# A 7x7 convolution by short transforms on one core: the weight transform as row-tiled pairs of 49-row matmuls

## Chip, core and metric

The kernel runs on one core of a Trainium2 chip. The metric is the device time of one execution in microseconds (us); less is better. TensorE is called PE in the profile (its weight loads PEld), VectorE DVE, ScalarE ACT, GpSimd POOL, and SyncE, which here only issues transfers, SP.

## The reference

The reference convolves an image x of 224 x 224 pixels and 96 channels (bf16) with a 7 x 7 filter w of 96 x 96 channels. It does so circularly, by Fourier transforms over the image plane:

```python
wp = jnp.pad(w, ((0, H - K), (0, W - K), (0, 0), (0, 0)))
Xf = rfft2(x.astype(float32), axes=(1, 2))
Wf = rfft2(wp.astype(float32), axes=(0, 1))
Yf = jnp.einsum('bhwi,hwio->bhwo', Xf, Wf)
y = irfft2(Yf, s=(H, W), axes=(1, 2)).astype(bfloat16)
```

The output has the shape of x.

## The kernel before

**The method.** The kernel doesn't use the large transform. Along the height it cuts the image into 8 blocks of 28 rows, each with 6 rows of halo, and takes a real transform of length 34 in each block: 17 frequencies, s = 0 to 16. Along the width it convolves directly, with 7 taps, two output columns at a time, in a form that replaces products by sums of inputs and sums of taps. So the weights are needed once per frequency, per part (up to three combinations of the real and imaginary part; such a combination is a "slot", 50 in all) and per tap or sum of taps (10), as matrices of 96 x 96: the tensor WF, [96 input channels, 50 slots, 10 taps, 96 output channels].

**The stages.**

1. Transform of x (`a_jobs`, `f_jobs`): matmuls with strips of x as weights and the table Fm moving, copied out of PSUM into xf.
2. Transform of w (`prep_jobs`): makes WF from w. This is the stage that the change rewrites.
3. Sums of the transformed inputs (`jit`), on VectorE, into J.
4. Products (`b_round`): for each strip t (seven strips of 32 image columns) and each frequency s, 36 or so matmuls of 96 rows, with J or xf as weights and WF moving. ScalarE, VectorE and GpSimd combine the results into yf, which goes to a scratch tensor in DRAM.
5. Back transform (`c_jobs`): reads the scratch, matmuls with the table Gm, copies to yo, stores the output.

**The transform of w.** SP loads w as a matrix wq with one row per tap position (49 rows, PW) and 96 x 96 columns (input channel times output channel). A second copy lies right below it, at row 49, shifted by half the output channels (48 columns), so that wq has 98 rows (PW2). For an output channel o, the weights of a matmul are the columns o, o + 96, o + 192 and so on: 128 columns with a step of 96 elements, of which the first 96 are the input channels. Columns past the matrix hold the table Em and zeros, so that these extra reads meet defined numbers. The moving operand is Em, a table of sine values times a mask over taps. It has two halves: half 0 is zero in rows 49 to 97, half 1 is zero in rows 0 to 48. One matmul with all 98 rows (line 332) so makes the columns of output channel o from the upper copy and of o + 48 from the lower. The slots are made in six groups (PGRP). Group 0 (two frequencies) is made with 49-row matmuls of 50 moving columns, eight to a PSUM bank. Groups 1 to 5 (three frequencies each) take 98-row matmuls of 120 columns, four to a bank, so 48 matmuls and 12 banks per group. After each bank, `evac` copies 480 elements per partition into WF, choosing VectorE or ScalarE by a running estimate of their loads. The third slot of a frequency isn't made by a matmul; it is the difference of two others (`diff`), on VectorE.

**What sets the order.** All instructions of an engine run in the order in which they are written; the wrapper `_Ordered` (lines 76 to 91) sees to it, and all of them carry the number of its line 86 in the profile. The prologue (lines 651 to 665) runs 16 jobs of the x transform, four of group 0, and then mixes them. Groups 1 to 5 are lists of jobs that `pace` (line 673) feeds into `b_round` at two points of each round, so that a list is used up evenly between a first and a last point:

```python
for gi in range(1, len(PGRP)):
    add(2 * PGRP[gi - 1][0], 2 * PGRP[gi - 1][1] - 1, prep_jobs(gi))
```

A list of a group has 12 matmul jobs (one bank each) and then three differences. PSUM has eight banks, which all jobs and rounds take in turn (`bank`); a round takes two.

**The tables.** Lines 209 to 265 compute Fm and Em. GpSimd makes the index ramps and zeroes the end of wq (line 232). VectorE reduces the angles, ScalarE takes the sines (`sin_q`), GpSimd masks the first (lines 240 and 241), and VectorE writes Fm (line 256), after it has computed the tap mask mk and its two halves mk2 (lines 252 to 255). Then it writes Em (lines 263 to 265). On SP the transfers are queued in this order: the first strips of x, the first copy of w, two more strips of x, the second copy of w (lines 176 to 185). A dummy matrix wu of zeros feeds 24 matmuls that keep TensorE busy from 1.05 us on.

Of the kernel before, what the change touches and what calls it, by code (L numbers as in the profile page):

```python
# [10 lines left out]
ALU = mybir.AluOpType  # L11
ACTF = mybir.ActivationFunctionType

KT = 7
# [11 lines left out]
NB = 8  # L26
POS = TW + HALO
NTAP = 10
TAPS = ((7, 8, 9, 6), (0, 2, 4, 6), (1, 3, 5))
NSLOT = 2 + 3 * (NS - 1)  # L30
# [18 lines left out]
def slot(s, part):  # L49
    return part if s == 0 else 2 + 3 * (s - 1) + part  # L50
# [3 lines left out]
def kernel(  # L54
# [7 lines left out]
    _, H, W, C = x.shape  # L62
# [4 lines left out]
    R = HB + PAD  # L67
    PW = KT * KT
    FR = 2 * NS
    PW2 = 2 * PW  # L70
    C2 = C // 2
    CG = ((0, 3), (3, 3), (6, 2))
    SYNC = mybir.DependencyInfo(mybir.DependencyClass.Sync, mybir.DependencyReason.DATA)
# [19 lines left out]
    VE, SE, GE, TE, DE = (_Ordered(e) for e in (nc.vector, nc.scalar, nc.gpsimd, nc.tensor, nc.sync))  # L93
# [9 lines left out]
    def bank():  # L103
        return pools["psb"].tile([128, 512], F32, name="pb")
# [5 lines left out]
    def apart(key, zone, r):  # L110
        for z, q in parts.setdefault(key, []):
            if z != zone and q.engine != r.ins.engine:
                tc.declare_no_dep(r.ins, q, reason="disjoint parts of one tile")
        parts[key].append((zone, r.ins))
        return r

    def evac(out_ap, in_ap, n):
        if tail[0]:
            return tail_evac(out_ap, in_ap, n)
        cv, ca = 180 + 1.0 * n, 160 + 0.85 * n  # L120
        if load["v"] + cv <= load["a"] + ca:
            load["v"] += cv
            return VE.tensor_copy(out=out_ap, in_=in_ap)
        load["a"] += ca
        return SE.copy(out=out_ap, in_=in_ap)

    def tail_evac(out_ap, in_ap, n):
        tail[0] += 1
        return VE.tensor_copy(out=out_ap, in_=in_ap) if tail[0] % 2 else SE.copy(out=out_ap, in_=in_ap)

    def dma(out_ap, in_ap):
        return DE.dma_start(out=out_ap, in_=in_ap)

    WF = cpool.tile([128, NSLOT, NTAP, C], BF16, name="WF")
# [4 lines left out]
    Fm = cpool.tile([R, 2, NS, JG], BF16, name="Fm")  # L139
# [9 lines left out]
    stmp = stmp_cm.__enter__()  # L149
    wqx = wtmp.tile([128, C - 1 + 127 * C + 1], BF16, name="wq")  # L150
    wq = wqx[0:PW2]
    Em = wqx[0:PW2, C * C:C * C + 2 * NSLOT * NTAP].rearrange("p (h a t) -> p h a t", h=2, a=NSLOT)
    XHW = PAD * C + 32
    xh_bufs = [J_bufs[2][0:R, i * XHW:(i + 1) * XHW] for i in range(2)]
    for xb in xn_bufs:
# [13 lines left out]
    def load_x(c):  # L169
        t, k = divmod(c, 4)  # L170
        h, jg = divmod(k, 2)
        load_rows(xn_bufs[c % NXN], jg, t * 2 * TW + h * PXC, PXC)

    wsrc = w.rearrange("kh kw i o -> (kh kw) (i o)")
# [5 lines left out]
    for h in range(2):  # L180
        if h:
            for c in range(2, NXN):
                load_x(c)
        for p0, p1 in ((0, 48), (48, PW)):
            dma(wq[h * PW + p0:h * PW + p1, 0:C * C - h * C2], wsrc[p0:p1, h * C2:])

    wu = cpool.tile([128, 128], BF16, name="wu")
    wur = wu[:].unsqueeze(1).to_broadcast([128, 4, 128])
# [8 lines left out]
    def ftile(shape):  # L197
        ntmp[0] += 1
        return stmp.tile(shape, F32, name=f"ct{ntmp[0]}")
# [4 lines left out]
    def floor_div(out_ap, in_ap, d):  # L204
        VE.tensor_scalar(out=out_ap, in0=in_ap, scalar1=1.0 / d, scalar2=-(d - 1) / (2.0 * d), op0=ALU.mult, op1=ALU.add)
        VE.tensor_single_scalar(out=out_ap, in_=out_ap, scalar=MAGIC, op=ALU.add)
        VE.tensor_single_scalar(out=out_ap, in_=out_ap, scalar=MAGIC, op=ALU.subtract)
# [2 lines left out]
    VE.memset(pi_t[:], math.pi)  # L210
    dmy = ftile([128, 1])
    SE.activation(out=dmy[:], in_=pi_t[:], func=ACTF.Sin, bias=0.0, scale=0.0)

    def sin_q(q):
        fl = ftile(list(q.shape))
        floor_div(fl[:], q, Q)
        VE.scalar_tensor_tensor(out=q, in0=fl[:], scalar=-float(Q), in1=q, op0=ALU.mult, op1=ALU.add)
        return SE.activation(out=q, in_=q, func=ACTF.Sin, bias=pi_t[:q.shape[0], :], scale=-2.0 * math.pi / Q)

    a2 = ftile([R, NS, 2]); ph2 = ftile([R, NS, 2]); nrj = ftile([R, JG])  # L220
    a3 = ftile([PW2, NS, 2]); ph3 = ftile([PW2, NS, 2])
    pw_i = ftile([PW2, 1]); thp = ftile([PW2, 1]); twp = ftile([PW2, 1]); hf = ftile([PW2, 1])
    twc = ftile([PW2, KT]); mk = ftile([PW2, NTAP]); mk2 = ftile([PW2, 2, NTAP])
    iota(a2[:], [[2, NS], [0, 2]])
    iota(ph2[:], [[0, NS], [17, 2]], base=17)
    iota(nrj[:], [[-B, JG]], cm=1)
# [2 lines left out]
    iota(ph3[:], [[0, NS], [-17, 2]], base=17)  # L229
    iota(twc[:], [[1, KT]])  # L230

    GE.memset(wqx[0:PW2, C * C + 2 * NSLOT * NTAP:], 0.0)
    VE.memset(a2[:, 0, 1:2], 34.0)
    VE.memset(ph2[:, 0, 1:2], 17.0)
    VE.tensor_scalar(out=nrj[:], in0=nrj[:], scalar1=0.0, scalar2=float(L - 1), op0=ALU.max, op1=ALU.min)
    qf = ftile([R, JG, NS, 2])
# [5 lines left out]

    VE.memset(a3[:, 0, 1:2], 34.0)
    VE.memset(ph3[:, 0, 1:2], 17.0)
    VE.tensor_single_scalar(out=hf[:], in_=pw_i[:], scalar=float(PW), op=ALU.is_ge)
    VE.scalar_tensor_tensor(out=pw_i[:], in0=hf[:], scalar=-float(PW), in1=pw_i[:], op0=ALU.mult, op1=ALU.add)
    floor_div(thp[:], pw_i[:], KT)
    VE.scalar_tensor_tensor(out=twp[:], in0=thp[:], scalar=-float(KT), in1=pw_i[:], op0=ALU.mult, op1=ALU.add)
    qe = ftile([PW2, NS, 2])
    VE.scalar_tensor_tensor(out=qe[:], in0=a3[:], scalar=thp[:, 0:1], in1=ph3[:], op0=ALU.mult, op1=ALU.add)  # L250
    sin_q(qe[:])
    VE.tensor_scalar(out=mk[:, 0:KT], in0=twc[:], scalar1=twp[:, 0:1], scalar2=None, op0=ALU.is_equal)
    VE.tensor_tensor(out=mk[:, KT:NTAP], in0=mk[:, 0:6:2], in1=mk[:, 1:6:2], op=ALU.add)
    VE.tensor_scalar(out=mk2[:, 1], in0=mk[:], scalar1=hf[:, 0:1], scalar2=None, op0=ALU.mult)
    VE.tensor_tensor(out=mk2[:, 0], in0=mk[:], in1=mk2[:, 1], op=ALU.subtract)
    VE.tensor_copy(out=Fm.rearrange("p r s j -> p j s r"), in_=qf[:])
    pe3 = ftile([PW2, NSLOT])
    pv = pe3[:, 2:].rearrange("p (s r) -> p s r", r=3)
    VE.tensor_copy(out=pe3[:, 0:2], in_=qe[:, 0, :])
# [1 line left out]
    VE.tensor_tensor(out=pv[:, :, 1], in0=qe[:, 1:, 1], in1=qe[:, 1:, 0], op=ALU.subtract)  # L261
    VE.tensor_tensor(out=pv[:, :, 2], in0=pv[:, :, 0], in1=pv[:, :, 1], op=ALU.subtract)
    for k0, k1 in ((0, slot(PGRP[0][1], 0)), (slot(PGRP[0][1], 0), NSLOT)):
        VE.tensor_tensor(out=Em[:, :, k0:k1], in0=pe3[:, k0:k1].unsqueeze(1).unsqueeze(3).to_broadcast([PW2, 2, k1 - k0, NTAP]),
                         in1=mk2[:].unsqueeze(2).to_broadcast([PW2, 2, k1 - k0, NTAP]), op=ALU.mult)

    def build_g(nj):
        PG = nj * FR
# [36 lines left out]
    def prep_jobs(gi):  # L305
        s0, s1 = PGRP[gi]
        ns = s1 - s0
        full = gi == 0
        if full:
            ncol = NSLOT_OF(s0, s1) * NTAP  # L310
        else:
            ncol = 2 * ns * NTAP
        nb = C // NB
        hb = NB // 2
        assert NB * ncol <= 512 and C2 % hb == 0

        def mk_(ob):
            def f():
                pw = bank()
                if full:  # L320
                    pv_ = pw[:, 0:NB * ncol].rearrange("p (o q) -> p o q", q=ncol)
                    ev = Em[0:PW, 0, slot(s0, 0):slot(s0, 0) + ncol // NTAP, :].rearrange("p a t -> p (a t)")
                    for k in range(NB):
                        o = ob * NB + k
                        TE.matmul(pv_[:, k], lhsT=wqx[0:PW, o:o + 127 * C + 1:C], rhs=ev, start=True, stop=True)
                    wv = WF[0:C, slot(s0, 0):slot(s0, 0) + ncol // NTAP].rearrange("i a t o -> i (a t) o")
                    apart(("W", gi), ob // 2, evac(wv[..., ob * NB:(ob + 1) * NB], pv_[0:C].rearrange("i o q -> i q o"), NB * ncol))
                    return
                pv_ = pw[:, 0:NB * ncol].rearrange("p (k h q) -> p k h q", h=2, q=ncol)
                ev = Em[:, :, slot(s0, 0):slot(s1 - 1, 2) + 1, :].rearrange("p h (s r) t -> p h s (r t)", r=3)[:, :, :, 0:2 * NTAP]  # L330
                for k in range(hb):
                    o = ob * hb + k
                    TE.matmul(pv_[:, k], lhsT=wqx[0:PW2, o:o + 127 * C + 1:C], rhs=ev, start=True, stop=True)
                pv_ = pv_[0:C]
                o0, o1 = ob * hb, (ob + 1) * hb
                wv = WF[0:C, slot(s0, 0):slot(s1 - 1, 2) + 1].rearrange("i (s r) t (h o) -> i s (r t) h o", r=3, h=2)
                apart(("W", gi), ob, evac(wv[:, :, 0:2 * NTAP, :, o0:o1],
                      pv_.rearrange("i k h (s q) -> i s q h k", s=ns), NB * ncol))
            return f

        def diff(s):
            def f():
                load["v"] += 60 + C * NTAP / 1.92
                w0, w1, w2 = (WF[0:C, slot(s, r)].rearrange("i t o -> i (t o)") for r in range(3))
                VE.tensor_tensor(out=w2, in0=w0, in1=w1, op=ALU.subtract)
            return f
        return [mk_(ob) for ob in range(nb)] + ([] if full else [diff(s) for s in range(s0, s1)])

    def NSLOT_OF(s0, s1):
        return slot(s1 - 1, 2) + 1 - slot(s0, 0)  # L350
# [301 lines left out]
    p0 = prep_jobs(0)  # L652
# [52 lines left out]
    for r in range(NS + LAG):  # L705
# [26 lines left out]
        for t in range(2):  # L732
            s = r - LAG * t
# [14 lines left out]
    for t in range(2, NT):  # L748
# [11 lines left out]
        k1 = 2 * NS if t < TL else 2 * NS - 6  # L760
        k0 = 10 if t == 2 else 3
# [44 lines left out]
    for _ in range(WARM):  # L806
        TE.matmul(live[order[7]].rearrange("p (a b) -> p a b", a=3), lhsT=wu[:, 0:M4], rhs=wu[:].unsqueeze(1).to_broadcast([128, 3, 128]),
                  start=False, stop=False)
    LF = 4
    for i, (g, q) in enumerate(order):  # L810
# [3 lines left out]
        k = i + 8 - LF  # L814
# [37 lines left out]
```

## Time and profile before

| | |
|---|---|
| median of three runs | 291.96 us (291.68 to 292.47) |
| the profiled execution, its own time | 292.68 us |
| its span, first to last instruction | 291.0 us |
| mean granted clock of TensorE | 0.965 |
| busy: PE, DVE, ACT, POOL | 272.5, 229.6, 195.8, 113.1 us |
| weight-transform matmuls, group 0 (49 rows, 50 columns) | 96, from 14.57 us on |
| weight-transform matmuls, groups 1 to 5 (98 rows, 120 columns) | 240, from 27.0 to 83.3 us |
| copies of 480 elements into WF on ACT, mean | 56, 579 ns |
| the same on DVE, mean | 4, 643 ns |
| zeroing the end of wq on POOL | 1, 1.83 us |

A line of the profile names the engine, the operation, what it writes and reads, and how often; then the time. [...]A line of the timeline gives the start and the length of a stretch of like instructions and their number. In square brackets stands the idle time before it and what ended it; that is inferred, and can name another engine than the true one. "PEclk" or the number after the busy times in a table of windows is the clock that TensorE was granted, 1.00 being full.

### The profile page before, as it was taken

What the parts mean: (1) busy time and instruction counts of PE and PEld (TensorE: products, weight loads), DVE (VectorE), ACT (ScalarE), POOL (GpSimd) and SP (SyncE); (2) the same over time, 40 slices, a digit from 0 to 9 for tenths busy, and PEclk for the clock granted to TensorE, in tenths of its full rate; (3) what the DMA queues carried; (4) which work ended last, traced back from release to release, by engine and by line L of the source; (5) the groups of instructions that cost most, each with busy time, mean ns of one, the idle gap of its engine ahead of it and who ended that gap; (6) DMA issues with size and microseconds to landing.
All of it is one profiled execution on the core that took longest, in us unless ns stands there. A gap on an engine that the chain in (4) does not pass through costs nothing.

```text
span 291.0 us, 11983 instructions
## 1 busy us (share of the span) xinstructions
PE 272.5 (94%) x5010; PEld 244.2 (84%) x5010; DVE 229.6 (79%) x472; ACT 195.8 (67%) x488; POOL 113.1 (39%) x151
## 2 busy tenths in 40 slices
PE   8598998999999998999899998999999999999982
PEld 3488988999999997888899987898988989888761
DVE  7847399997978889979977888787998779786723
ACT  2555994958774555886788867897788865677113
POOL 6824022348446565332643227222552323422100
PEclk9955899999999999999999999999999999999997
DMA  8894142111111299977567685778539543887756
GB/s 195 132 236 124 51 112 84 45 43 44 43 43 49 87 277 193 274 225 216 170 190 206 194 243 144 204 210 237 169 95 267 148 131 108 198 245 197 201 108 189
DMA packets 45830, 46.04 MB, mean 158 GB/s; under 512 B 33626, under 2 KB 34758, under 8 KB 45678
## 3 DMA queue, kind: packets, MB, share of 16 engines
q1 hardware_dynamic: 43488, 43.21, 55.3%
q10 hardware_dynamic: 2288, 2.06, 2.5%
q8 instruction: 39, 0.64, 1.0%
q14 instruction: 15, 0.12, 0.2%
HBM read 23.92 MB, written 21.33 MB: 156 GB/s over the span
## 4 chain that ended last, share of the span: by engine, by line
PE 65%; DVE 14%; DMA 5%; issue 5%; POOL 4%; ACT 4%; SPq 1%; DVEq 0%; ACTq 0%; POOLq 0%
PE pb L86 65%; DVE J L86 6%; POOL ct L86 3%; DVE v L86 2%; DMA tt<-scr 2%; DVE u L86 2%; DMA xf<-scrb 2%; ACT xf L86 2%; DVE WF L86 1%; DVE yf L86 1%; DVE ct L86 1%; ACT WF L86 1%; POOL yf L86 1%; SPq L86 1%; DMA scrb<-yf 1%
## 5 line engine op out<-in xcount | busy, mean ns | idle before, releaser
L86 PE MATMUL pb<-WF,J 96*128 96x96 bf16 x2898 | 169.2, 206 | 2.8 <-DVE J L86 1.4
L86 PEld LDWEIGHTS <-J 96*128 96x128 bf16 (+1 forms) x2910 | 142.9, 98 | 18.5 <-issue 10.1
L86 POOL TENSOR_TENSOR yf<-v,u 128x384 bf16<-128x384 f32 x85 | 83.7, 999 | 144.9 <-issue 97.3
L86 ACT CAST xf<-pb 96x408 bf16<-96x408 f32 (+3 forms) x150 | 68.4, 481 | 11.3 <-PE pb L86 9.2
L86 ACT CAST yo<-pb 84x384 bf16<-84x384 f32 (+1 forms) x144 | 61.4, 481 | 6.4 <-PE pb L86 3.4
L86 DVE TENSOR_TENSOR J<-xf 96x1824 bf16<-96x1824 bf16 (+1 forms) x84 | 64.4, 806 | 0.0
L86 PE MATMUL pb<-WF,xf 96*128 96x96 bf16 x952 | 60.7, 207 | 2.1 <-DVE WF L86 2.0
L86 PE MATMUL pb<-Fm,xn 118*128 118x136 bf16 (+3 forms) x576 | 52.1, 216 | 2.4 <-DVE u L86 1.9
L86 PEld LDWEIGHTS <-xf 96*128 96x128 bf16 x952 | 47.5, 98 | 2.6 <-issue 1.5
L86 PEld LDWEIGHTS <-xn 118*128 118x128 bf16 x576 | 34.3, 100 | 3.8 <-issue 2.9
L86 PE MATMUL pb<-tt,Gm 102*84 102x384 bf16 (+1 forms) x144 | 35.8, 329 | 0.6 <-DVE v L86 0.4
L86 ACT CAST WF<-pb 96x480 bf16<-96x480 f32 (+1 forms) x62 | 30.7, 570 | 5.1 <-PE pb L86 5.1
L86 PE MATMUL pb<-wq 98*128 98x120 bf16 (+1 forms) x336 | 26.5, 234 | 2.3 <-POOL ct L86 2.3
L86 DVE TENSOR_TENSOR J<-J 96x912 bf16<-96x912 bf16 (+1 forms) x42 | 28.3, 674 | 0.0
L86 PEld LDWEIGHTS <-wq 98*128 98x128 bf16 (+1 forms) x336 | 23.8, 152 | 3.8 <-POOL ct L86 2.4
L86 POOL COPY xf<-xf 96x816 bf16<-96x816 bf16 (+3 forms) x16 | 16.7, 1073 | 0.0
L86 DVE TENSOR_TENSOR yf<-v,u 128x384 bf16<-128x384 f32 x27 | 15.5, 575 | 0.9
L86 PEld LDWEIGHTS <-Gm 102*84 102x84 bf16 (+1 forms) x144 | 11.4, 114 | 3.1 <-issue 0.6
L86 PE MATMUL pb<-wu 128*112 128x384 bf16 (+1 forms) x60 | 13.0, 380 | 1.1 <-DVE ct L86 1.1
L86 PEld LDWEIGHTS <-wu 128*112 128x112 bf16 (+1 forms) x60 | 7.3, 124 | 6.4 <-issue 2.5
L86 DVE TENSOR_TENSOR WF<-WF 96x960 bf16<-96x960 bf16 x15 | 11.0, 787 | 0.1
L86 ACT CAST tt<-pb 112x384 bf16<-112x384 f32 x8 | 3.6, 479 | 9.7 <-PE pb L86 9.6
(388 smaller groups left out, 210.2 us busy)
## 6 DMA issues: line engine op xcount, KB each, us to landing
xn<-in_x_dram SPq DMA_DIRECT2D x28, 336.0 KB
scr<-yf SPq DMA_DIRECT2D x30, 288.0 KB
tt<-scr SPq DMA_DIRECT2D x24, 288.0 KB
out_dram<-yo SPq DMA_DIRECT2D x24, 252.0 KB
tt<-scr SPq DMA_DIRECT2D x12, 192.0 KB
out_dram<-yo SPq DMA_DIRECT2D x12, 168.0 KB
out_dram<-tt SPq DMA_DIRECT2D x4, 336.0 KB
scr<-yf SPq DMA_DIRECT2D x6, 192.0 KB
```

Source lines behind the costliest of these rows:

```text
L86: r = fn(*a, **k)
```

## The change

The second copy of w now begins at row 64 (WR) and isn't shifted. Rows 49 to 63 are left out, so that wq and the tables beside it have 64 + 49 = 113 rows. Em has one half only, the same values in rows 0 to 48 and 64 to 112.

Groups 1 to 5 are made by jobs that fill two PSUM banks (`two`). A job makes eight output channels in one bank from rows 0 to 48, and the eight that lie 48 further in the other bank from rows 64 to 112. Its matmuls take turns between the two: each has 49 rows, 128 weight columns with the step of 96, and 60 moving columns, and is given its place in the array (row 0 or row 64). So a group has 96 matmuls in 48 pairs instead of 48 matmuls, and six jobs of two banks instead of twelve of one. Group 0 is unchanged (`one`).

In the tables, the zeros at the end of wq are written by ScalarE from wu instead of by GpSimd's memset; the two halves of the mask are gone; and VectorE writes Fm before the tap mask.

```diff
-    PW2 = 2 * PW
+    WR = 64
+    PW2 = WR + PW
...
-    Em = wqx[0:PW2, C * C:C * C + 2 * NSLOT * NTAP].rearrange("p (h a t) -> p h a t", h=2, a=NSLOT)
+    Em = wqx[0:PW2, C * C:C * C + NSLOT * NTAP].rearrange("p (a t) -> p a t", a=NSLOT)
...
-            dma(wq[h * PW + p0:h * PW + p1, 0:C * C - h * C2], wsrc[p0:p1, h * C2:])
+            dma(wq[h * WR + p0:h * WR + p1, 0:C * C], wsrc[p0:p1])
...
+    zw = wqx[0:PW2, C * C + NSLOT * NTAP:]
+    SE.copy(out=zw, in_=wu[0:PW2, 0:1].to_broadcast(list(zw.shape)))
...
-    GE.memset(wqx[0:PW2, C * C + 2 * NSLOT * NTAP:], 0.0)
...
-    VE.tensor_single_scalar(out=hf[:], in_=pw_i[:], scalar=float(PW), op=ALU.is_ge)
-    VE.scalar_tensor_tensor(out=pw_i[:], in0=hf[:], scalar=-float(PW), in1=pw_i[:], op0=ALU.mult, op1=ALU.add)
+    VE.tensor_single_scalar(out=hf[:], in_=pw_i[:], scalar=float(WR), op=ALU.is_ge)
+    VE.scalar_tensor_tensor(out=pw_i[:], in0=hf[:], scalar=-float(WR), in1=pw_i[:], op0=ALU.mult, op1=ALU.add)
...
     sin_q(qe[:])
+    VE.tensor_copy(out=Fm.rearrange("p r s j -> p j s r"), in_=qf[:])
     VE.tensor_scalar(out=mk[:, 0:KT], in0=twc[:], scalar1=twp[:, 0:1], scalar2=None, op0=ALU.is_equal)
     VE.tensor_tensor(out=mk[:, KT:NTAP], in0=mk[:, 0:6:2], in1=mk[:, 1:6:2], op=ALU.add)
-    VE.tensor_scalar(out=mk2[:, 1], in0=mk[:], scalar1=hf[:, 0:1], scalar2=None, op0=ALU.mult)
-    VE.tensor_tensor(out=mk2[:, 0], in0=mk[:], in1=mk2[:, 1], op=ALU.subtract)
-    VE.tensor_copy(out=Fm.rearrange("p r s j -> p j s r"), in_=qf[:])
...
-        VE.tensor_tensor(out=Em[:, :, k0:k1], in0=pe3[:, k0:k1].unsqueeze(1).unsqueeze(3).to_broadcast([PW2, 2, k1 - k0, NTAP]),
-                         in1=mk2[:].unsqueeze(2).to_broadcast([PW2, 2, k1 - k0, NTAP]), op=ALU.mult)
+        VE.tensor_tensor(out=Em[:, k0:k1], in0=pe3[:, k0:k1].unsqueeze(2).to_broadcast([PW2, k1 - k0, NTAP]),
+                         in1=mk[:].unsqueeze(1).to_broadcast([PW2, k1 - k0, NTAP]), op=ALU.mult)
...
-                pv_ = pw[:, 0:NB * ncol].rearrange("p (k h q) -> p k h q", h=2, q=ncol)
-                ev = Em[:, :, slot(s0, 0):slot(s1 - 1, 2) + 1, :].rearrange("p h (s r) t -> p h s (r t)", r=3)[:, :, :, 0:2 * NTAP]
-                for k in range(hb):
-                    o = ob * hb + k
-                    TE.matmul(pv_[:, k], lhsT=wqx[0:PW2, o:o + 127 * C + 1:C], rhs=ev, start=True, stop=True)
-                pv_ = pv_[0:C]
-                o0, o1 = ob * hb, (ob + 1) * hb
-                wv = WF[0:C, slot(s0, 0):slot(s1 - 1, 2) + 1].rearrange("i (s r) t (h o) -> i s (r t) h o", r=3, h=2)
-                apart(("W", gi), ob, evac(wv[:, :, 0:2 * NTAP, :, o0:o1],
-                      pv_.rearrange("i k h (s q) -> i s q h k", s=ns), NB * ncol))
...
+        def two(ob):
+            def f():
+                obs = (ob, ob + nb // 2)
+                pv_ = [bank()[:, 0:NB * ncol].rearrange("p (o q) -> p o q", q=ncol) for _ in obs]
+                ev = Em[:, slot(s0, 0):slot(s1 - 1, 2) + 1, :].rearrange("p (s r) t -> p s (r t)", r=3)[:, :, 0:2 * NTAP]
+                for k in range(NB):
+                    for h, b in enumerate(obs):
+                        o, p0 = b * NB + k, h * WR
+                        TE.matmul(pv_[h][:, k], lhsT=wqx[p0:p0 + PW, o:o + 127 * C + 1:C], rhs=ev[p0:p0 + PW],
+                                  start=True, stop=True, tile_position=(p0, 0), skip_group_check=True)
+                wv = WF[0:C, slot(s0, 0):slot(s1 - 1, 2) + 1].rearrange("i (s r) t o -> i s (r t) o", r=3)[:, :, 0:2 * NTAP]
+                for h, b in enumerate(obs):
+                    apart(("W", gi), b, evac(wv[..., b * NB:(b + 1) * NB],
+                          pv_[h][0:C].rearrange("i k (s q) -> i s q k", s=ns), NB * ncol))
+            return f
...
-        return [mk_(ob) for ob in range(nb)] + ([] if full else [diff(s) for s in range(s0, s1)])
+        return [one(ob) for ob in range(nb)] if full else [two(ob) for ob in range(nb // 2)] + [diff(s) for s in range(s0, s1)]
```

More of the change, by code (lines that the diff above doesn't have):

```diff
@@ L222 @@
     pw_i = ftile([PW2, 1]); thp = ftile([PW2, 1]); twp = ftile([PW2, 1]); hf = ftile([PW2, 1])
-    twc = ftile([PW2, KT]); mk = ftile([PW2, NTAP]); mk2 = ftile([PW2, 2, NTAP])
+    twc = ftile([PW2, KT]); mk = ftile([PW2, NTAP])
     iota(a2[:], [[2, NS], [0, 2]])
@@ L308, in prep_jobs, with one @@
         full = gi == 0
[L309 to L312, printed above, removed]
+        ncol = NSLOT_OF(s0, s1) * NTAP if full else 2 * ns * NTAP
         nb = C // NB
-        hb = NB // 2
-        assert NB * ncol <= 512 and C2 % hb == 0
-        def mk_(ob):
+        assert NB * ncol <= 512 and nb % 2 == 0
+        def one(ob):
             def f():
                 pw = bank()
[L320 to L328, printed above, removed]
-                pv_ = pw[:, 0:NB * ncol].rearrange("p (k h q) -> p k h q", h=2, q=ncol)
-                ev = Em[:, :, slot(s0, 0):slot(s1 - 1, 2) + 1, :].rearrange("p h (s r) t -> p h s (r t)", r=3)[:, :, :, 0:2 * NTAP]
-                for k in range(hb):
-                    o = ob * hb + k
-                    TE.matmul(pv_[:, k], lhsT=wqx[0:PW2, o:o + 127 * C + 1:C], rhs=ev, start=True, stop=True)
-                pv_ = pv_[0:C]
-                o0, o1 = ob * hb, (ob + 1) * hb
-                wv = WF[0:C, slot(s0, 0):slot(s1 - 1, 2) + 1].rearrange("i (s r) t (h o) -> i s (r t) h o", r=3, h=2)
-                apart(("W", gi), ob, evac(wv[:, :, 0:2 * NTAP, :, o0:o1],
-                      pv_.rearrange("i k h (s q) -> i s q h k", s=ns), NB * ncol))
@@ new lines, in f @@
+                pv_ = pw[:, 0:NB * ncol].rearrange("p (o q) -> p o q", q=ncol)
+                ev = Em[0:PW, slot(s0, 0):slot(s0, 0) + ncol // NTAP, :].rearrange("p a t -> p (a t)")
+                for k in range(NB):
+                    o = ob * NB + k
+                    TE.matmul(pv_[:, k], lhsT=wqx[0:PW, o:o + 127 * C + 1:C], rhs=ev, start=True, stop=True)
+                wv = WF[0:C, slot(s0, 0):slot(s0, 0) + ncol // NTAP].rearrange("i a t o -> i (a t) o")
+                apart(("W", gi), ob // 2, evac(wv[..., ob * NB:(ob + 1) * NB], pv_[0:C].rearrange("i o q -> i q o"), NB * ncol))
@@ new lines, in one @@
+            return f
[4 more added lines that the diff above has]
+                ev = Em[:, slot(s0, 0):slot(s1 - 1, 2) + 1, :].rearrange("p (s r) t -> p s (r t)", r=3)[:, :, 0:2 * NTAP]
+                for k in range(NB):
+                    for h, b in enumerate(obs):
[6 more added lines that the diff above has]
+                          pv_[h][0:C].rearrange("i k (s q) -> i s q k", s=ns), NB * ncol))
```

## The prediction

> **What bounds the kernel now.** I read the chain of waits first, then the table of windows, then the timeline around the weight matmuls.
>
> ```profile
> PE 65%; DVE 14%; DMA 5%; issue 5%; POOL 4%; ACT 4%; SPq 1%; DVEq 0%; ACTq 0%; POOLq 0%
> ```
>
> TensorE is 65% of the chain, so whether a change to TensorE counts depends on the stage. The weight groups are made in the first 84 us. The windows (us, then busy time of PE, PEld, DVE, ACT, POOL, then the granted clock) are:
>
> ```profile
> 14.50:26.40 11.90, 11.11 (x128) 9.44 (x128) 6.14 (x12) 6.35 (x14) 2.01 (x7) 0.51 0.86 200
> 26.40:36.00 9.60, 9.57 (x135) 9.47 (x136) 4.57 (x6) 8.29 (x21) 2.68 (x3) 0.72 0.21 65
> 36.00:50.00 14.00, 12.42 (x231) 11.69 (x229) 13.90 (x27) 10.11 (x26) 3.03 (x3) 1.00 0.36 102
> 50.00:61.00 11.00, 11.00 (x237) 10.88 (x236) 10.22 (x20) 7.82 (x18) 4.94 (x5) 1.00 0.09 30
> 61.00:80.00 19.00, 17.88 (x392) 17.58 (x391) 17.06 (x33) 14.09 (x32) 10.13 (x11) 1.00 0.14 50
> ```
>
> The clock is half from 14.5 us until within the second window. From 26 to 50 us ACT and DVE share the limit; from 50 us on TensorE is never idle for long. [...]Weight loads of one full-clock stretch (start, length, count):
>
> ```profile
> 49.63 0.82 PEld L86 LDWEIGHTS <-wq 98*128 98x128 bf16 x12
> 50.37 0.84 PEld L86 LDWEIGHTS <-J 96*128 96x128 bf16 x18
> 51.16 0.40 PEld L86 LDWEIGHTS <-xf 96*128 96x128 bf16 x8
> ```
>
> Twelve weight-group matmuls take 50.37 - 49.63 = 0.74 us, 0.062 each; eighteen convolution matmuls 0.79, 0.044 each. At half clock:
>
> ```profile
> 26.95 2.04 PEld L86 LDWEIGHTS <-wq 98*128 98x128 bf16 x20
> 28.93 1.38 PEld L86 LDWEIGHTS <-xn 118*128 118x128 bf16 x12
> ```
>
> Here it is 1.98/20 = 0.099 us. Group 0, which already uses 49 rows, stands between other matmuls at half clock:
>
> ```profile
> 17.09 0.58 PEld L86 LDWEIGHTS <-xn 118*128 118x128 bf16 x6
> 17.88 0.57 PEld L86 LDWEIGHTS <-wq 49*128 49x128 bf16 x8 [0.21 <-issue]
> 18.50 0.58 PEld L86 LDWEIGHTS <-xn 118*128 118x128 bf16 x6
> ```
>
> Its loads are (0.57 - 0.15)/7 = 0.060 us apart with only 50 moving columns and the slow clock[...]. And there is a hole of 0.21 us before the stretch, which the 98-row matmuls don't have.
>
> [...]above, convolution loads start every 0.044 us while each matmul runs 0.206. [...]VectorE's first 118x136 step at 3.11 us took 1.40 where the next two took 0.24, beside GpSimd's memset of 2.59 to 4.42.
>
> **The change, part by part.**
>
> *Number of matmuls.* Groups 1 to 5 go from 240 to 480, in 240 pairs. If the two loads of a pair run together, a pair costs the 0.061 of one strided load; if one after the other, 0.122[...]. No 64-row pair is in this trace, so these are the bounds. I take 0.061[...]. From 49.2 to 84 us there are 144 matmuls in twelve stretches now; in the program order after the change 144 pairs in nine. Pairs: 144 x (0.061 - 0.062) = -0.15 us.
>
> *Changes of mode.* Program order after the change has 14 stretches of pairs between full-row matmuls. The price comes from the output stage, where two matmuls with 56 weight columns stand where elsewhere stand two of 84:
>
> ```profile
> 132.19 0.46 PE L86 MATMUL pb<-WF,J 96*128 96x96 bf16 x7
> 132.48 0.49 PE L86 MATMUL pb<-tt,Gm 102*84 102x384 bf16 x2
> 132.81 0.93 PE L86 MATMUL pb<-WF,J 96*128 96x96 bf16 x18
> ```
>
> ```profile
> 135.65 0.46 PE L86 MATMUL pb<-WF,J 96*128 96x96 bf16 x7
> 136.04 0.51 PE L86 MATMUL pb<-tt,Gm 68*56 68x384 bf16 x2
> 136.48 0.94 PE L86 MATMUL pb<-WF,J 96*128 96x96 bf16 x18
> ```
>
> From the seven to the eighteen it is 0.62 us against 0.83: 0.21 us in and out, at full clock. Group 0 at half clock: 0.79 for six matmuls of 0.112 (the twelve above: (1.38 - 0.15)/11) leaves 0.12, and 0.62 for eight of 0.060 leaves 0.14, together 0.26. Nine stretches after 49.2 us: 9 x 0.21 = +1.89, all on TensorE's path. Sum there: +1.74 us.
>
> *26 to 49 us.* 96 pairs in five stretches, two of 24 pairs. The first is at half clock[...]: 20 x (0.061 - 0.099) = -0.76, with 0.26 for the mode -0.50; the other four +0.84. Together +0.34 at most; ACT and DVE limit much of it, so +0.34 is taken, 0 to 0.8 being the bounds.
>
> *Order of jobs.* A group is 6 pair jobs and 3 differences instead of 12 and 3, so differences come due earlier. This bears on one stall: TensorE stands 1.26 us before 49.21 us for VectorE's first difference, which took 1.40 us beside a GpSimd sum. In the new VectorE order two differences precede the u step and follow the J steps directly. Gain 0 to 1.0; I take 0.4, since the pairs make TensorE arrive later anyway.
>
> *Evacuation.* Twelve copies of 480 elements per group stay; but two banks come free together at a job's end, and a 32-matmul stretch leaves four copies. ACT then needs 0.3 + 4 x 0.49 = 2.3 us (its copies are three in 1.47), and TensorE's round is 2.16 + 4 x 0.061 + 0.21 = 2.6: covered. If not, the convolution banks queued behind wait. 0 to 0.6, taken 0.3.
>
> *Start.* GpSimd loses its 1.83-us memset, which frees VectorE by 1.40 - 0.24 = 1.16 us; the masks lose two small steps and the table Em half its size (1.39 us now). ScalarE gains a 113x2572 copy: its rows give some 0.87 ns an element, so 2.4 us in its idle 3.10 before 5.39 us; without that cover the sine and Fm would wait the excess. So Fm is done about 2 us sooner. But the chain into the weights is
>
> ```profile
> 14.32 1.98 SPq L86 DMA_DIRECT2D xn<-in_x_dram  x3
> 14.54 1.58 PEld L86 LDWEIGHTS <-wq 49*128 49x128 bf16 x25 [2.43 <-POOL ct L86]
> ```
>
> The load waits for the w transfer (and the memset, long done). SP's next transfer, which waits for that same w transfer, issues at 14.32; so w landed then, and the named POOL step is a coincidence. Fm sooner only lengthens the idle before it: 0. The w transfers keep their place on SP and 48 columns more in the second: 0.
>
> Sum: 1.74 + 0.34 - 0.4 + 0.3 = +1.98 us. On the profiled execution, 292.68 us (a span of 291.0 and 1.7 around it), that is 294.7; its time stands 0.72 above the median of 291.96, so against the median 294.0.
>
> **Rivals.** *The loads of a pair run one after the other*[...]. For it: every strided load here comes 0.06 after the one before. Then 144 x 0.060 = 8.6 more after 49.2 us; before it 96 x 0.061 = 5.9, of which some 2.5 hide in TensorE's stalls there (1.26 and smaller ones): 294.0 + 12.0 = 306. *The drain is covered*: pairs at the least distance of 0.050 save 144 x 0.011 = 1.6 and give it back as drains: 292.4. *Faster:* the pair at 0.050 and a mode change between two row tilings at half the price of the column one, 0.10. Then after 49.2 us 9 x (0.10 - 16 x 0.012) = -0.8, before it 0.3 - 0.9 with the difference: 290.6. It decides when 16 x (0.062 - pair) exceeds the drain; against it speaks group 0's 0.26.
>
> **How the numbers follow.** Pairs together with drains, 53%, 293.0 to 296.5; loads in turn, 27%, 303 to 309; covered, 12%; faster, 8%. The range 291.5 to 308 leaves out the fast case and the slowest end of the serial one. A difference of 0.3% (0.9 us) is about what a measurement of this kernel can tell from no change. Faster 0.08, same 0.13, slower 0.79.
>
> **What would show it.** Weight loads of a 32-matmul stretch at 49 to 84 us: 1.0 us for together, 1.95 for in turn, 0.8 for the floor. Before and after each, holes of 0.1 us. Group 0 still starting at 14.5 us, with Fm near 6.3 instead of 8.2. It is wrong if the half clock ends much earlier or later than about 31 us, or if ACT's copies make TensorE wait for banks.

## The result, and the profile after

The changed kernel takes 300.98 us (299.96 to 302.37 over four runs) where the kernel before takes 292.01 (291.68 to 292.47) beside it: a ratio of 1.031, with a 95% interval of 1.026 to 1.036, or 9.0 us more. The forecast was 2.0 us more. The profiled execution took 299.96 us, with a span of 298.2 and a mean granted clock of 0.946, against 292.68, 291.0 and 0.965.

The table of windows of the changed kernel (us, then busy time of PE, PEld, DVE, ACT, POOL, then the granted clock, the DMA share and GB/s), in the stretches that the prediction showed of before:

```profile
14.50:26.40 11.90, 10.75 (x127) 9.22 (x127) 5.45 (x10) 5.75 (x13) 0.36 (x1) 0.60 0.97 183
26.40:36.00 9.60, 8.85 (x157) 8.34 (x156) 5.76 (x8) 7.99 (x20) 3.02 (x3) 0.50 0.21 52
36.00:50.00 14.00, 13.67 (x292) 12.98 (x290) 12.32 (x25) 10.63 (x27) 2.53 (x3) 0.95 0.43 125
50.00:61.00 11.00, 10.48 (x247) 9.87 (x247) 9.68 (x17) 7.09 (x17) 3.83 (x4) 1.00 0.08 30
61.00:80.00 19.00, 17.91 (x347) 17.48 (x345) 15.47 (x28) 9.81 (x22) 8.54 (x10) 0.73 0.09 33
```

Read the clock's column first. The half clock now fills the second window (0.50 where it was 0.72), reaches into the third, and comes back in the last (0.73 where it was 1.00). There TensorE does 347 matmuls in the 19 us that held 392, although the change adds matmuls. The same in the page's row of clock slices (7.5 us each), where the second dip is the "57" after a run of four nines:

```profile
PEclk9965599995799999999999999999999999999999
```

The trace dates the two half-clock stretches at 16.9 to 37.4 us and 68.1 to 78.3; before there was one, 14.6 to 31.7. By the page a matmul of 96 columns lasts 209 ns in the mean here, while such matmuls start 0.042 us apart at full clock (median), so what one costs is counted from start to start. The weight loads around one stretch of pairs at full clock (start, length, count):

```profile
56.34 0.35 PEld L87 LDWEIGHTS <-J 96*128 96x128 bf16 x7
56.77 1.07 PEld L87 LDWEIGHTS <-wq 49*128 49x128 bf16 x32
57.88 0.20 PEld L87 LDWEIGHTS <-J 96*128 96x128 bf16 x4
```

Thirty-two loads start within 57.88 - 56.77 = 1.11 us, of which 0.16 is the way out. The single starts in the trace lie 0.0307 us apart: 0.061 for a pair. And the round after another stretch, on PE, DVE and DVE:

```profile
65.87 0.93 PE L87 MATMUL pb<-WF,J 96*128 96x96 bf16 x18 [1.09 <-DVE v L87]
```

```profile
63.92 1.43 DVE L87 TENSOR_TENSOR WF<-WF 96x960 bf16<-96x960 bf16 x1
65.28 0.54 DVE L87 SCALAR_TENSOR_TENSOR v<-tt__1416,pb 128x384 f32<-128x384 f32 x1
```

TensorE stands 1.09 us for the bank that VectorE's v reads, and v stands behind a difference of 1.43 us. Of the chain of waits the page now follows only the part from 91 us on, so its shares can't be set against those of before. I compared positions instead: the start of the n-th matmul that doesn't belong to the weight transform, after minus before, is +1.0 us at 26 us, +1.2 at 34, between +0.8 and +3.1 from 47 to 63, +3.8 at 67, +7.1 at 79, +8.0 at 85, +6.9 at 95 and +8.2 at 99, and it stays between 8.1 and 8.7 to 267 us. So the loss arises while the weights are made.

### The profile page after: what moved, and what is told of

It is laid out like the page before. It is cut to its first block, busy times and chain, and to the rows that moved or that the text cites. A ratio compares the mean times of both kernels' runs of the same rounds, so it can differ in the third digit from the quotient of the medians.

```text
span 298.2 us, 12460 instructions
## 1 busy us (share of the span) xinstructions
PE 279.4 (94%) x5250; PEld 250.0 (84%) x5250; DVE 231.0 (77%) x472; ACT 198.0 (66%) x487; POOL 110.5 (37%) x150
## 4 chain that ended last, share of the span: by engine, by line
PE 47%; DVE 12%; issue 3%; DMA 2%; ACT 1%; POOL 1%; DVEq 0%; ACTq 0%; SPq 0%
PE pb L87 47%; DVE J L87 5%; DVE v L87 2%; DVE yf L87 2%; DVE u L87 2%; DMA xf<-scrb 1%; POOL xf L87 1%; DMA scrb<-yf 1%; ACT xf L87 0%; DVE WF L87 0%; POOL yf L87 0%; ACT yo L87 0%; DVE tt L87 0%; DVEq L847 0%; ACT tt__4778 L87 0%
## 5 line engine op out<-in xcount | busy, mean ns | idle before, releaser
L87 PE MATMUL pb<-WF,J 96*128 96x96 bf16 x2898 | 172.4, 209 | 4.2 <-DVE J L87 2.3
L87 PEld LDWEIGHTS <-J 96*128 96x128 bf16 (+1 forms) x2910 | 145.7, 99 | 19.2 <-issue 9.3
L87 ACT CAST xf<-pb 96x408 bf16<-96x408 f32 (+3 forms) x148 | 67.5, 476 | 12.3 <-PE pb L87 10.1
L87 PE MATMUL pb<-WF,xf 96*128 96x96 bf16 x952 | 61.8, 209 | 1.1 <-DVE WF L87 1.1
L87 PEld LDWEIGHTS <-xf 96*128 96x128 bf16 x952 | 48.6, 100 | 1.5 <-ACT ct L87 0.8
L87 PE MATMUL pb<-wq 49*128 49x60 bf16 (+1 forms) x576 | 24.8, 228 | 4.1 <-DMA wq<-in_w_dram 3.9
L87 PEld LDWEIGHTS <-wq 49*128 49x128 bf16 x576 | 22.4, 159 | 6.9 <-issue 5.6
L87 PE MATMUL pb<-wu 128*112 128x384 bf16 (+1 forms) x60 | 14.1, 403 | 1.1 <-DVE ct L87 1.1
L87 DVE TENSOR_TENSOR WF<-WF 96x960 bf16<-96x960 bf16 x15 | 14.7, 1008 | 0.0
L87 DVE CAST xf<-pb 96x408 bf16<-96x408 f32 (+1 forms) x20 | 9.4, 510 | 4.1 <-PE pb L87 4.0
```

Of the source, the lines that this page charges most:

```text
L87: r = fn(*a, **k)
```

## The experiments

Times are medians beside runs of the kernel before on the same chip. Mode changes and drains are the author's names for the time added at the two ends of a stretch of pairs, 0.18 us in the changed kernel (worked out below); what TensorE does in that time isn't shown. Theory A: these ends cost what was forecast, and the rest comes from two other effects of the change, the pace of its two-bank jobs and the half clock. Theory B: the pairs themselves are slow (loads in turn, or dearer ends). The clock theory of the expectations is the author's guess that the pairs, with 60 columns a matmul, bring the second half-clock stretch; e4_wide tests it.

**The edits of the tables alone** (e1_tables), on the kernel before:

```diff
...
+    SE.copy(out=zw, in_=wu[0:PW2, 0:1].to_broadcast(list(zw.shape)))
-    GE.memset(wqx[0:PW2, C * C + 2 * NSLOT * NTAP:], 0.0)
...
     sin_q(qe[:])
+    VE.tensor_copy(out=Fm.rearrange("p r s j -> p j s r"), in_=qf[:])
...
-    VE.tensor_copy(out=Fm.rearrange("p r s j -> p j s r"), in_=qf[:])
```

> The kernel before with only the change's edits to the tables: ScalarE instead of GpSimd zeroes the end of the w matrix, and Fm is written ahead of the tap mask. If the w transfer sets the start of group 0 (the prediction's reading), the time stays within 0.3% of 292 us, group 0 starts at 14.3 to 14.7 us and Fm is ready some 2 us sooner. If the table edits are what delays group 0 after the change (15.65 instead of 14.57 us there), group 0 starts near 15.6 here too and the time is about 293.

Measured: 291.56 against 292.13, ratio 0.998 (0.996 to 1.001). Group 0 starts at 14.70 us, and Fm is made at 6.26 us where before has 8.22. The tables cost and gain nothing that can be measured, and by this profile they are not what delays group 0 after the change.

**The order of jobs alone** (e2_jobs): 98-row matmuls as before, in jobs of two banks, six jobs and three differences to a group, as after.

```diff
...
+                obs = (ob, ob + nb // 2)
+                pws = [pw, bank()]
...
                 for k in range(hb):
-                    o = ob * hb + k
-                    TE.matmul(pv_[:, k], lhsT=wqx[0:PW2, o:o + 127 * C + 1:C], rhs=ev, start=True, stop=True)
+                    for i, b in enumerate(obs):
+                        o = b * hb + k
+                        TE.matmul(pvs[i][:, k], lhsT=wqx[0:PW2, o:o + 127 * C + 1:C], rhs=ev, start=True, stop=True)
...
-        return [mk_(ob) for ob in range(nb)] + ([] if full else [diff(s) for s in range(s0, s1)])
+        return [mk_(ob) for ob in range(nb)] if full else [mk_(ob) for ob in range(nb // 2)] + [diff(s) for s in range(s0, s1)]
```

> The kernel before, its full 98-row matmuls kept, but in jobs of two banks (six jobs and three differences for a group, as after the change). Clock theory[...]: nothing of that here, so 291 to 293 us and a granted clock of about 0.965. Job theory (the coarser jobs, the copies two by two and the earlier differences cause the stalls of 1 us and more seen after the change): 296 us or more, with the stalls at the same places.

Measured: 296.16 against 292.13, ratio 1.0146 (1.009 to 1.020), +4.3 us without one pair in it. A list of nine entries is used up over the same points as one of fifteen, so three rounds running now take four banks of weights where four rounds took three. ScalarE's copies of one such stretch grow from 1.47 us to 1.93. What it does to TensorE, in the timeline of e2_jobs:

```profile
69.02 1.08 PE L86 MATMUL pb<-wq 98*128 98x120 bf16 x15 [0.57 <-DVE u L86]
```

```profile
78.20 0.59 PE L86 MATMUL pb<-wq 98*128 98x120 bf16 x7 [0.97 <-DVE v L86]
...
81.38 0.64 PE L86 MATMUL pb<-wq 98*128 98x120 bf16 x8 [0.44 <-DVE u L86]
```

These waits stand inside a stretch: its first matmuls have run, and the next needs a bank that VectorE's u or v, by the profile, has still to read. In each of the three the u or v ends at most 0.05 us before the matmul starts. A fourth hole inside a stretch, 0.46 us at 52.75, ends with a copy of ScalarE into WF instead. Before, no such hole lies inside a stretch. I listed all places between 45 and 100 us where two consecutive matmuls start more than 0.4 us apart:

| kernel | holes | their sum, us | of it inside weight stretches |
|---|---|---|---|
| before | 4 | 3.6 | 0 |
| e2_jobs | 9 | 7.2 | 3.1 |
| e5_difflast | 8 | 6.2 | 1.8 |
| e6_spread | 5 | 4.3 | 1.0 |
| e4_wide | 8 | 6.4 | 2.4 |
| after | 5 | 3.9 | 0.5 |

**The loops of a pair swapped** (e3_halves), on the changed kernel: eight matmuls in rows 0 to 48, then eight in rows 64 to 112.

```diff
-                for k in range(NB):
-                    for h, b in enumerate(obs):
+                for h, b in enumerate(obs):
+                    for k in range(NB):
```

> The changed kernel, but a job makes its eight matmuls in rows 0 to 48 first and its eight in rows 64 to 112 after them. If two strided loads run together only when neighbours go to different halves, a matmul costs 0.060 us in place of 0.0305, a stretch of 32 takes 1.9 us in place of 0.95, and the time is 308 to 314 us (240 x 0.06 = 14 us more, less what stalls hide). If the loads run ahead over more than one matmul, the stretch stays near 1.0 us and the time near 301.

Measured: 303.8 us, ratio 1.039 (1.034 to 1.045). Its loads, to be set beside the 1.07 us above:

```profile
53.36 1.39 PEld L87 LDWEIGHTS <-wq 49*128 49x128 bf16 x32
```

The starts are 0.041 us apart, between 0.031 (alternating) and 0.060 (one half of the rows only, as in group 0). So loads that alternate between the two halves start about twice as often as loads into one half, and less often than that when eight of a half follow each other. Neither expectation had that middle value, nor the time.

**More columns per pair** (e4_wide): each matmul of a pair moves its 60 columns twice; what the second copy writes is overwritten by the next matmul.

```diff
-                        TE.matmul(pv_[h][:, k], lhsT=wqx[p0:p0 + PW, o:o + 127 * C + 1:C], rhs=ev[p0:p0 + PW],
+                        r = 1 if k == NB - 1 else 2
+                        TE.matmul(pv_[h][:, k:k + r].rearrange("p r (s q) -> p r s q", s=ns), lhsT=wqx[p0:p0 + PW, o:o + 127 * C + 1:C],
+                                  rhs=ev[p0:p0 + PW].unsqueeze(1).to_broadcast([PW, r, ns, 2 * NTAP]),
```

> The changed kernel, but each matmul of a pair moves 120 columns in place of 60 (the last of a bank still 60); the second 60 are written over the place of the next output channel and overwritten by its matmul, so the result is that of the changed kernel. At full clock this costs nothing[...]. Clock theory:[...] the half clock near 68 to 78 us goes and the first one ends earlier, 294 to 296 us with a granted clock of 0.96 or more. Job and drain theory: nothing changes or it gets slower, 300 us or more, clock 0.945.

Measured: 299.18 us, ratio 1.023 (1.019 to 1.028), mean clock 0.969. More work on TensorE, and less time than the changed kernel. Its windows:

```profile
26.40:36.00 9.60, 9.10 (x169) 8.68 (x170) 5.48 (x8) 7.75 (x19) 3.02 (x3) 0.72 0.27 70
...
61.00:80.00 19.00, 16.65 (x413) 16.09 (x410) 16.94 (x30) 10.97 (x26) 9.13 (x11) 1.00 0.14 50
```

The clock is as before the change, 0.72 and 1.00, and the last window holds 413 matmuls instead of 347. All four runs have a mean clock of 0.968 or 0.969, those of the changed kernel 0.937 to 0.952. That the second half-clock stretch goes when the matmuls of a pair move 120 columns in place of 60 is thereby shown. At full clock the wider columns add next to nothing to a stretch of 32: 1.13 us (56.00 to 57.13) where the changed kernel has 1.11. The clock came as the clock theory expected, the time (294 to 296 us) did not: the clock is only a part of the loss.

**The differences last and together** (e5_difflast), on e2_jobs: is it a difference ahead of v that makes the pace dear?

```diff
...
+        df = [diff(s) for s in range(s0, s1)]
+        return [mk_(ob) for ob in range(nb // 2)] + [lambda: None, lambda: None, lambda: [f() for f in df]]
```

> Full 98-row matmuls in jobs of two banks as in the run e2_jobs (296.2 us), but the three differences of a group run together at the group's last point, as before the change. If the lone difference that runs ahead of VectorE's v step (1.42 us beside a GpSimd sum) makes the stalls of 1 to 1.4 us, they go: 293 us or less. If the stretches of four banks make them (TensorE waits for a bank to be copied), 295 to 296 us.

Measured: 295.06 against 291.39, ratio 1.0144 (1.009 to 1.020), the same as e2_jobs. The waits move, to a round that now wants the weights of the late differences (DVE, then PE):

```profile
61.18 2.31 DVE L86 TENSOR_TENSOR WF<-WF 96x960 bf16<-96x960 bf16 x3
```

```profile
62.41 0.33 PE L86 MATMUL pb<-WF,xf 96*128 96x96 bf16 x4 [0.52 <-DVE WF L86]
```

A single early difference is a part of one wait, but not what makes the order cost 4 us.

**The two-bank jobs spread** (e6_spread), on e2_jobs: an empty entry after each job makes a list of fifteen again.

```diff
...
+        return [f for ob in range(nb // 2) for f in (mk_(ob), lambda: None)] + [diff(s) for s in range(s0, s1)]
```

> Full 98-row matmuls in jobs of two banks, six empty places put between them, so that a group's list has 15 places as before the change, and banks and differences come due as before (alternating four and two banks in place of three). If the pace of the list is the cause of the 4.2 us of e2_jobs, 292 to 293 us. If it is that two banks come free together, 295 us or more.

Measured: 292.54 against 291.39, ratio 1.0045 (1.003 to 1.006): 1.3 us of the 4.3 remain (the difference, 3.0, has some 1.6 of uncertainty). One hole inside a stretch is left in its timeline:

```profile
67.84 0.34 PE L86 MATMUL pb<-wq 98*128 98x120 bf16 x3 [0.73 <-DVE u L86]
```

**The pairs spread likewise** (e7_pairspread), on the changed kernel:

```diff
...
+        return [f for ob in range(nb // 2) for f in (two(ob), lambda: None)] + [diff(s) for s in range(s0, s1)]
```

> The changed kernel with its list stretched to 15 places in the same way. If pace, drains and clock add up as read so far (4.2, 1.7 and 2.2 us of the 9.0), the pace goes, two more drains a group come in (about 0.2 us each), and whether the half clock returns is open: 295 to 297 us. If the pairs themselves are what stalls, 300 us or more.

Measured: 294.07 us in one run at a mean clock of 0.958, and 300.7 to 302.9 in three at 0.926 to 0.933. With so wide a spread no ratio is given, and nothing is concluded from this kernel.

**Spread pairs with more columns** (e9_pairspread_wide): the edit of e4_wide on e7_pairspread.

> As e7_pairspread, and each matmul of a pair moves 120 columns as in e4_wide (the second 60 overwritten by the next channel's matmul). Clock theory: the granted clock is 0.96 or more, and the drains alone are left over the kernel before, 19 stretches of 0.2 us less what is hidden: 294 to 295.5 us. If the wide matmul costs time of its own, it is slower than e7_pairspread.

Measured: 295.42 against 291.39, ratio 1.015 (1.011 to 1.020), and all four runs between 294.96 and 296.68, at a mean clock of 0.961 to 0.968. The last window is at full clock; one short half-clock stretch is left in the profiled run, from 43.4 to 46.9 us:

```profile
61.00:80.00 19.00, 19.00 (x468) 18.42 (x467) 16.91 (x34) 12.55 (x29) 9.58 (x11) 1.00 0.14 50
```

Against e6_spread, the same order with 98-row matmuls, this is 0.0108 of 291.4, or 3.1 us for nineteen stretches of pairs: 0.17 each, with the wider columns in it and some 1.4 of uncertainty in the 3.1.

**A busier TensorE at the start** (e8_warm): can the half clock at the start be shortened? On e1_tables; twelve matmuls of zeros fill the wait for w (nothing reads their bank), and group 0 moves its columns twice.

```diff
...
+                        r = 1 if k == NB - 1 else 2
+                        TE.matmul(pv_[:, k:k + r], lhsT=wqx[0:PW, o:o + 127 * C + 1:C],
+                                  rhs=ev.unsqueeze(1).to_broadcast([PW, r, ncol]), start=True, stop=True)
...
+    pwu = bank()
+    for _ in range(12):
+        TE.matmul(pwu[:].rearrange("p (a b) -> p a b", a=4), lhsT=wu[:, 0:128], rhs=wur, start=True, stop=True)
```

> The kernel before with the table edits of e1_tables, and the array kept busy around group 0: twelve 512-column matmuls of zeros into a bank that nobody reads fill the wait for w, and group 0's matmuls move 100 columns in place of 50 (the second 50 overwritten by the next channel's). Clock theory: the half clock of 14.6 to 31.7 us goes, the matmuls of 136 columns cost 0.058 us there in place of 0.112, and 2 to 3 us are saved: 289 to 290 us with a clock above 0.98. If the clock doesn't follow what the array is moving, 291 to 292 us and a clock of 0.965.

Measured: 291.55 against 291.33, ratio 0.9987 (0.997 to 1.001): no gain. The profiled run had half clock only from 19.4 to 29.6 us and took 290.36; over all runs the time went from 288.5 (clock 0.982) to 294.2 (0.967). It shortens nothing reliably.

**The first copy of w alone on the transfers** (e10_wfirst): on e8_warm, strips 3 and 4 of x and the second copy of w are issued only when the first 48 rows of the first copy have landed; four matmuls of zeros stand in place of twelve.

```diff
...
+            if not h and p0 == 0:
+                first = r
+        if not h:
+            late.append(first)
...
+        for q in late:
+            tc.add_manual_dep(r.ins, q.ins.name, SYNC, reason="after the first copy of w")
```

> As e8_warm, but the transfers of the third and fourth strip of x and of the second copy of w start only when the first copy of w has landed, and four matmuls of zeros fill the wait. If these transfers are what holds back the first copy (it lands at 14.3 us in the kernel before), group 0 starts near 11.5 us and the time is 286 to 288 us. If the following strips of x then come too late for the jobs between group 0's, the gain is lost there: 289 to 291 us.

Measured: 293.09 against 291.33, ratio 1.006 (1.004 to 1.009). Its window ahead of group 0, and SP's next issue:

```profile
11.00:14.50 3.50, 0.97 (x6) 0.23 (x3) 1.79 (x5) 0.46 (x2) 2.99 (x9) 1.00 0.12 21
```

```profile
15.15 1.42 SPq L86 DMA_DIRECT2D xn<-in_x_dram  x4
```

The transfers were 0.12 busy at 21 GB/s (e8_warm: 0.80 at 154 in the same window), and the 48 rows still landed only at 15.15 us. The expectation missed: the transfers issued after w are not what holds it back here. By the trace the last packet of the strips issued ahead of it ends at 8.1 us, and from then on w is alone here; yet its packets, one row of 18 KB each, that start between 8.5 and 10.6 us take 2.3 us in the median, where they take 2.1 in e8_warm beside the strips. The last of them starts at 13.47 us. Why a row takes so long, and the last ones start so late, is open.

## Why the prediction was right in direction and short by 7 us

The measured time lies in none of the forecast cases: it is above 296.5, the end of "pairs together with drains", and below 303, where "loads in turn" begins. The whole range, 291.5 to 308, holds it only because it reaches out to that second case, which didn't occur. The direction came from a term that held, the mode changes; most of the loss came from elsewhere. By its own steps:

**Pairs.** Forecast 0.061 us a pair, measured 0.061. The rival "loads in turn" (306 us, 27%) falls, with that half of theory B, and so does "faster", which needed 0.050. That the two loads of a pair run together was the author's estimate, shown by no trace of before; the 0.0307 us between starts bears it out for loads that alternate (0.041 in e3_halves, where they don't). The 0.050, called the least distance in the prediction, is an estimate too: twice the 0.025 us at which matmuls of 32 and of 40 columns start in before (medians at full clock). That none can come closer wasn't shown. Since a 98-row matmul makes the same two output channels in 0.062, there was nothing to win.

**Mode changes.** Forecast 0.21 us a stretch. At full clock the changed kernel has 0.138 from start to start on the way in, where 0.043 is usual, and 0.152 on the way out instead of 0.063: 0.095 + 0.089 = 0.18. Nine of them make 1.7 us; the term was 1.89. By the medians, e4_wide minus e2_jobs is 0.0086 of 292, or 2.5 us for fourteen stretches, with some 2 us of uncertainty. The size of the term stands, and the rival of a covered drain and the dearer ends of theory B fall, by the trace above all. That pairs of rows would cost about what the two matmuls with 56 weight columns cost in the output stage (0.21) was the author's estimate; here it came out near.

**The step that failed: evacuation.** It said that a stretch leaves ScalarE four copies, 2.3 us against a TensorE round of 2.6: "covered", 0.3, at most 0.6. The copies were sized right (1.93 us), but the question was put to one engine only. With three rounds running at four banks, the stretch takes banks that have not yet been read, mostly by VectorE's u and v, and TensorE stops in mid-stretch: in e2_jobs 2.7 us of such holes end with u or v and 0.46 with a copy of ScalarE. e2_jobs prices the order of jobs at +4.3 us where the prediction had -0.4 + 0.3, and e6_spread shows that some 3.0 of it is the burst: the same jobs over fifteen places. Which of VectorE's steps is the one that comes late, no run separates; e5_difflast rules out the position of the differences alone. In the changed kernel itself little of this is left: the one hole inside a stretch, 0.45 us from start to start, ends with ScalarE's copy, and VectorE's v ends the 1.09 us after a stretch shown above.

```profile
54.59 0.62 PE L87 MATMUL pb<-wq 49*128 49x60 bf16 x15 [0.24 <-ACT WF L87]
```

**Order of jobs.** The stall that this term looked at did shrink, from 1.26 us to 0.31 (before 50.04 us in the changed kernel), more than the 0.4 taken. What it left out are the new waits elsewhere, which e2_jobs shows.

**The condition named and not priced: the clock.** "Wrong if the half clock ends much earlier or later than about 31 us": it ended at 37.4, and came again for 10.2 us. The prediction took the half clock as given, while the change itself moved it: between 61 and 80 us the clock is 0.73 with pairs of 60 columns and 1.00 with 120 (e4_wide). e4_wide against the changed kernel gives 0.0077 of 292, or 2.2 us, with some 1.8 of uncertainty; in the profiled runs its group 0 also began 0.6 us sooner. In the changed kernel's own trace the second half clock is larger: 97 matmuls of 96 columns start 0.080 us apart in it where 0.042 is usual, which makes 3.7 us. The position comparison agrees: +3.3 us between 67 and 79 us, with two stretches of pairs in it, where e4_wide has +0.4.

**The sum isn't a plain one.** In the changed kernel itself the holes between matmuls add only 0.3 us over before (3.9 against 3.6). The half clock from 68 to 78 us slows TensorE just where e2_jobs waits, so that, as I read it, VectorE catches up; in e4_wide, at full clock, the holes are back (at 67.6, 78.1 and 81.5 us). That 4.3 for the pace, 2.5 for the ends of the stretches and 2.2 for the clock add up to 9.0 confirms nothing: they are the steps of one path, from before over e2_jobs and e4_wide to after, and must add up. Along another path the shares would differ. In the changed kernel's own profile the second half clock is the largest part: 3.7 us, against 14 x 0.18 = 2.5 for the ends of the stretches and 0.3 for the holes.

**Start.** Fm comes sooner, as forecast: VectorE's three steps from 3.11 us take 0.76 us where they took 1.92 beside GpSimd's memset, the 1.16 of the forecast. ScalarE's copy of 2.32 us fits; no gain follows, since TensorE waits for w:

```profile
2.20 2.32 ACT L87 COPY wq<-wu 113x2572 bf16<-113x2572 bf16 x1
...
6.23 0.47 DVE L87 CAST Fm<-ct 118x136 bf16<-118x136 f32 x1
...
15.65 0.56 PE L87 MATMUL pb<-wq 49*128 49x50 bf16 x7 [3.89 <-DMA wq<-in_w_dram]
```

That group 0 began at 15.65 us and not at 14.57 the prediction didn't have. It took the issue of SP's next transfer for the landing of w, but the first copy of w comes as two transfers, of 48 rows and of the last row, and that issue waits for the 48 alone. By the trace these landed at 14.24 us before and 14.29 after; the last row landed at 14.44 before and at 15.51 after, and group 0 started then. In e3_halves the 48 rows are the late ones, at 15.74. The profiled runs of the five kernels with pairs start group 0 at 14.98 to 15.79, those of before and of the five others with 98-row matmuls and the same order of transfers (e1, e2, e5, e6, e8) at 14.52 to 14.99. With one profiled run each, whether the second copy's new place does this is open; the means of the two lots are 0.6 us apart, and that can be a part of the 9.

**26 to 49 us.** Forecast +0.34, between 0 and 0.8. The positions go from +1.0 at 26 us, which is the later start of group 0, to between +1.5 and +1.8 from 47 to 50 us, so 0.5 to 0.8 arose here, in one profiled run of each kernel. That a pair takes 0.061 at half clock too was the author's estimate; at half clock the matmuls of the changed kernel's pairs start 0.0305 us apart in the mean, again 0.061 a pair. The term wasn't tested alone.

No kernel here beats the one before: e1_tables and e8_warm are level with it.

## What to carry to other kernels

When a change makes jobs coarser, price its pace first: count how many PSUM banks a round now takes and ask which engines have to have read those banks, not whether the new copies fit in a round. Splitting rows into pairs that move half the columns each gained nothing here (0.061 us a pair, 0.062 for the 98-row matmul) and brought a second stretch of half clock, 10.2 us long. A change in how many columns TensorE's matmuls move has to be forecast with a clock of its own, not with that of the trace before: here the clock from 61 to 80 us fell from 1.00 to 0.73.

## What was not expected of the hardware

- The half-clock stretches that begin in the first 100 us last 3.41, 10.24, 13.65, 17.07, 20.48 or 23.89 us in the twelve profiles, close to whole multiples of the shortest. What begins and ends one isn't shown. That the second one goes when the matmuls of a pair move 120 columns is shown (e4_wide).
- Group 0's matmuls in the changed kernel, whose loads take 128 weight columns with a step of 96 elements, start 0.061 us apart at half clock and 0.059 at full clock (medians), where 96-column matmuls go from 0.080 to 0.042. Such loads in different halves of the rows start 0.0307 us apart if they alternate.
- In the profiles of before, the changed kernel, e2_jobs and e5_difflast every difference of 96x960 that starts while GpSimd's sum into yf runs takes 0.98 to 1.46 us, and every other one 0.64 to 0.66. Before has four of the long kind, the changed kernel and e2_jobs seven.
